# Turning the second group of v by DMA instead of on TensorE, with a split weight load, a wider first fold and later finish steps

## The chip, the cores and the metric

The kernel runs on one core of one Trainium2 chip. The metric is the device time of one execution in microseconds (us). A ratio is the mean time of one kernel's fast runs over that of the kernel before's fast runs of the same rounds, so it is not quite the ratio of the medians that are quoted. The kernel before was timed again with each batch: its medians were 722.87, 723.02 and 723.03 us, so the batches can be laid side by side. A transfer is said to land when the trace records its last completion. Half clock means stretches in which the trace's clock record of TensorE stands at 0.5. Counts of DMA packets by size are taken from the packet records of the traces; no view lists them by size.

## The reference, cut to what matters

```python
# B, N, C = 4, 6080, 256; D_ff = 2048; tau = 1; all float32
qn, kn = q / (norm(q, axis=1) + 1e-6), k / (norm(k, axis=1) + 1e-6)
a = softmax(kn.transpose(0, 2, 1) @ qn / tau)      # 256 x 256 for each b
x = (v @ a).reshape(B * N, C)
r = maximum(x @ w_in, 0)
out = (s * r * r + b) @ w_out
```

## The kernel before

The attention matrix is folded into the first weight, `wa = a @ w_in`, once for each of the four blocks b. After that the work runs over 48 groups of 512 rows of v. A step is one 128-wide part of D_ff: TensorE multiplies `wa` by the turned group `vT` (`mm1`), ScalarE takes the relu, VectorE or ScalarE squares, TensorE multiplies by `w_out`. So each group of v has to be turned first: 128x128 parts with rows and columns exchanged. In the lines below `h_ps` is the result of mm1, `r` its relu, `g` the square, `o_ps` the product with `w_out`, `u` a sum that VectorE makes from `o_ps`, `wa_ps` a piece of the folded weight and `s_ps` the product of k and q for the attention matrix.

```python
def transpose_v(g):                       # on TensorE: 8 transpositions and a copy
    ...
    for j in range(nj):
        for ch in range(CH):
            po(nc.tensor.transpose(vT_ps[:, ch, ts(j, P)], v16[:, j, ts(ch, P)], ident16))
    vT = vtpool.tile([P, CH, TG], FP16, tag="vT", name="vT")
    po(nc.vector.tensor_copy(out=vT[:, :, : nj * P], in_=vT_ps[:, :, : nj * P]))

def crossbar_v(g):                        # by DMA, from SyncE: 4 transfers
    ...
    for j in range(nj):
        po(nc.sync.dma_start_transpose(out=vT[:, :, ts(j, P)], in_=v16[:, j, :]))
```

Groups 0 and 1 are turned on TensorE, all later ones by DMA. The loads of v, w_in, w_out and nearly all of q and k are issued from GpSimd and share its queue; most of them cast from float32 to float16. Their order at the start:

```python
    # ... q and k of block 0 ...
    load_w_in(0, NW)                      # NW = 512
    load_v(0)
    load_w_in(NW, Dff)
    load_v(1)
    # ... w_out in four pieces, load_v(2), scalars; then v3, v4 and q, k of block 1
```

The first `wa` columns are made in pieces, and for later blocks the attention matrix is finished in ten operations placed by the list FIN; one of them, `join` (L266), adds two halves that were turned by DMA (`t_hi`, `t_lo`):

```python
    folds = [fold_both(0, P), fold_both(P, P)]
    folds += [fold_one(2 * P, NW - 2 * P, m) for m in range(CH)]
    ...
    FIN = (-12, 0, 3, 3, 5, 7, 13, 15, 17, 20)   # sqrt, norms, recip, exp, hi, lo, join, exps, exps, sums
```

Of the kernel before, what the change touches and what calls it, by code (L numbers as in the profile page):

```python
# [16 lines left out]
def kernel(  # L17
# [13 lines left out]
    P = 128  # L31

    B, N, C = q.shape
    Dff = moe_w_in.shape[1]
# [19 lines left out]
    def po(ins):  # L54

        tc.keep_in_program_order(ins)
        return ins
# [30 lines left out]
    def h_tile(name):  # L88
        return ps_h.tile([P, 2, TG], FP32, tag="h_ps", name=name)
# [19 lines left out]
    class Gram:  # L109
# [111 lines left out]
        def finish_ops(self):  # L221
# [77 lines left out]
            def scaled(f0, n, m, wa_ps):  # L299
                dst = self.wa[:, m, ds(f0, n)]  # L300
                if m == 0:
                    po(nc.scalar.mul(out=dst, in_=wa_ps, mul=st["rs"][:, m : m + 1]))
                else:
                    po(nc.vector.tensor_scalar_mul(
                        out=dst, in0=wa_ps, scalar1=st["rs"][:, m : m + 1]))

            def fold_mm(f0, n, m, wa_ps):
                for j in range(CH):
                    po(nc.tensor.matmul(wa_ps, st["e"][:, j, ts(m, P)],  # L309
                                        w_in16[:, j, ds(f0, n)],  # L310
                                        start=(j == 0), stop=(j == CH - 1)))

            def fold_both(f0, n):
                def f():

                    two = [self.bank("wa_ps", CH, C)[:, 0, :n], h_tile("wa_ps")[:, 0, :n]]
                    for m in range(CH):
                        fold_mm(f0, n, m, two[m])
                    for m in range(CH):
                        scaled(f0, n, m, two[m])  # L320
                return f

            def fold_one(f0, n, m):
                def f():
                    wa_ps = self.bank("wa_ps", CH, C).rearrange("p a c -> p (a c)")[:, :n]
                    fold_mm(f0, n, m, wa_ps)
                    scaled(f0, n, m, wa_ps)
                return f

            if self.b == 0:  # L330

                folds = [fold_both(0, P), fold_both(P, P)]
                folds += [fold_one(2 * P, NW - 2 * P, m) for m in range(CH)]
            else:
                folds = []
# [16 lines left out]
    def group(g):  # L352
        t0 = g * TG
        return t0, min(TG, NT - t0) // P
# [3 lines left out]
    def load_v(g):  # L358
        t0, nj = group(g)
        v16 = vpool.tile([P, TG // P, C], FP16, tag="v16", name="v16")  # L360
        po(nc.gpsimd.dma_start(  # L361
            out=v16[:, :nj, :],
            in_=v_flat[t0 : t0 + nj * P, :].rearrange("(p j) c -> p j c", j=nj)))
        v_tiles[g] = v16

    def transpose_v(g):
        _, nj = group(g)
        v16 = v_tiles.pop(g)
        vT_ps = ps_o.tile([P, CH, TG], FP16, tag="o_ps", name="vT_ps")
# [5 lines that stand above are left out]
        vT_tiles[g] = vT  # L375

    def crossbar_v(g):

        _, nj = group(g)
        v16 = v_tiles.pop(g)  # L380
# [3 lines that stand above are left out]
        vT_tiles[g] = vT  # L384
# [22 lines left out]
    NW = 512  # L407
    w_in_rows = moe_w_in.rearrange("(co p) f -> p co f", p=P)

    def load_w_in(f0, f1):  # L410
        po(nc.gpsimd.dma_start(out=w_in16[:, :, f0:f1], in_=w_in_rows[:, :, f0:f1]))

    load_w_in(0, NW)
    load_v(0)
    load_w_in(NW, Dff)
    w_out_rows = moe_w_out.rearrange("(fo p) d -> p fo d", p=P)
    load_v(1)

# [37 lines left out]
    fin = g0.finish_ops()  # L456
# [4 lines left out]
    keep_busy(4, w_in16[:, 0, :P], w_in16[:, 0, :NW])  # L461
    fin[5]()
    transpose_v(0)
    for f in fin[6:13]:
        f()


# [44 lines left out]
    def at_step(s, f):  # L512
        side.setdefault(int(s), []).append(f)


    FIN = (-12, 0, 3, 3, 5, 7, 13, 15, 17, 20)
    first_group = [b * N // TG for b in range(B)]
    FOLDS = (0, 0, 3, 4, 7, 8)
    for i, f in enumerate(fin[13:]):
        at_step(FOLDS[i], f)  # L520
    at_step(14, lambda: po(nc.vector.tensor_scalar_mul(
        out=s_out, in0=s_bc, scalar1=1.0 / (LAM * LAM))))
# [14 lines left out]
    for g in range(NG):  # L537
        if g >= 3:
            at_step(max(g - 4, 0) * FT + 2, lambda g=g: load_v(g))
        if g >= 1:  # L540
            if g == 1:
                at_step(12, lambda g=g: transpose_v(g))
            else:
                at_step((g - 2) * FT + 6, lambda g=g: crossbar_v(g))
    for b in range(1, B):
# [21 lines left out]
        def fin_step(gr=gr, s=w1 - fin_len):  # L567
            ops = gr.finish_ops()
            for i, f in enumerate(ops):
                at_step(int(s) + 1 + (FIN[i] if i < 10 else FIN[9] + 3 + (i - 10) * 3), f)  # L570
        at_step(w1 - fin_len - 12, fin_step)
# [224 lines left out]
    for s in range(NS + FT):  # L796
        g, m = divmod(s, FT)
# [66 lines left out]
```

## Time and profile before

| | before |
|---|---|
| time, median of 3 (range) | 722.93 us (722.61 to 723.24) |
| TensorE busy | 700.3 us of the 721.1 us span |
| VectorE, ScalarE busy | 626.3, 544.6 us |
| TensorE idle from 80 us to the end of the steady part | 1.7 us, once, near 164 us |

TensorE is the bound, so the useful question is where it stands still. Besides the lines that the prediction shows, one view is needed: the busy time of each engine in chosen stretches. Its columns are the stretch, its length, then busy us (number of instructions) of PE, PEld, DVE, ACT and POOL, the granted clock of TensorE as a share of full speed, the busy share of the DMA engines and GB/s. Of the kernel before:

```profile
50.00:60.00 10.00, 9.47 (x59) 5.66 (x58) 9.17 (x18) 9.76 (x11) 0.84 (x2) 1.00 1.02 155
60.00:80.00 20.00, 19.37 (x173) 13.47 (x171) 18.91 (x29) 18.08 (x25) 4.44 (x9) 1.00 1.01 167
```

In the stretch where the second group begins (51.8 us), TensorE, ScalarE and VectorE are all nearly full and the clock is full; the DMA engines are full as well (1.02).

### The profile page before, as it was taken

To read this page: it belongs to the slowest core of one execution; us is meant where nothing else is said; L and a number is where in the kernel's file an instruction comes from. 1 tells how busy PE (TensorE), PEld (TensorE's weight loads), DVE (VectorE), ACT (ScalarE), POOL (GpSimd) and SP (SyncE) were. 2 spreads that over 40 slices of the span, in tenths; PEclk is the share of its full clock that TensorE was granted. 3 is DMA by queue.
4 is the path that set the end of the run, shared out by engine and by line. 5 is a ranking of instruction groups with operands and counts; after the bars stand their busy time and mean duration, and the time that the engine had idled before them with its cause. 6 is when DMAs were issued, how large, how long until landed. Compare 5 with 4: busy or idle time off the path is not lost.

```text
span 721.1 us, 17651 instructions
## 1 busy us (share of the span) xinstructions
PE 700.3 (97%) x7485; PEld 505.4 (70%) x7485; DVE 626.3 (87%) x880; ACT 544.6 (76%) x589; POOL 109.1 (15%) x188
## 2 busy tenths in 40 slices
PE   4799999999999999999999999999999999999998
PEld 3556777776677777777677777777668777777777
DVE  4779999988889999999788898999888888888886
ACT  4479877887777777788777777878877777777875
POOL 4522331201101222110210222110000000000000
PEclk9999999999999999999999999999999999999999
DMA  9999998637474989353864777953423333321202
GB/s 236 208 259 140 176 174 141 110 103 126 97 118 105 154 146 141 80 118 78 144 134 89 129 135 131 159 93 83 103 64 78 89 75 74 97 59 45 83 30 75
DMA packets 89519, 84.27 MB, mean 117 GB/s; under 512 B 59648, under 2 KB 64576, under 8 KB 89440
## 3 DMA queue, kind: packets, MB, share of 16 engines
q0 software_dynamic: 25792, 43.40, 37.2%
q1 hardware_dynamic: 63072, 38.43, 21.3%
q8 instruction: 59, 0.97, 0.6%
q10 hardware_dynamic: 576, 1.31, 0.5%
q14 instruction: 20, 0.16, 0.1%
HBM read 78.91 MB, written 24.90 MB: 144 GB/s over the span
## 4 chain that ended last, share of the span: by engine, by line
PE 90%; DMA 5%; DVE 1%; ACT 1%; POOL 1%; issue 1%; DVEq 0%; ACTq 0%; POOLq 0%
PE h_ps L604 44%; PE o_ps L772 39%; PE s_ps L142 4%; PE wa_ps L309 2%; DMA qk<-in_q_dram 2%; DMA w_in<-in_moe_w_in_dram 1%; DMA qk<-in_k_dram 1%; ACT r L614 1%; DMA t_lo<-s_lo 1%; POOL qk L126 1%; PE o_ps L650 0%; PE o_ps L676 0%; ACT g L625 0%; DVE o_sb L632 0%; DVE S L698 0%
## 5 line engine op out<-in xcount | busy, mean ns | idle before, releaser
L614 ACT ACTIVATE r<-h_ps 128x1024 f16<-128x1024 f32 (+1 forms) x384 | 387.8, 1014 | 148.2 <-PE h_ps L604 146.3
L604 PE MATMUL h_ps<-vT,wa 128*128 128x512 f16 (+7 forms) x1632 | 451.9, 364 | 0.6 <-ACT r L614 0.4
L772 PEld LDWEIGHTS <-S 128*128 128x128 f16 x2944 | 197.9, 98 | 85.1 <-issue 0.4
L772 PEld LDWEIGHTS <-g 128*128 128x128 f16 x2208 | 155.0, 98 | 74.1
L627 DVE TENSOR_TENSOR g<-r 128x2048 f16<-128x2048 f16 (+2 forms) x150 | 174.5, 1164 | 16.9 <-ACT r L614 16.9
L772 PE MATMUL o_ps<-T,S 128*128 128x128 f16 x2208 | 183.2, 219 | 0.3 <-DVE S L698 0.2
L604 PEld LDWEIGHTS <-wa 128*128 128x128 f16 x1632 | 136.1, 98 | 23.0 <-issue 2.8
L772 PE MATMUL o_ps<-w_out,g 128*128 128x128 f16 x1472 | 134.2, 219 | 2.0 <-DVE u L632 2.0
L632 DVE SCALAR_TENSOR_TENSOR o_sb<-o_ps,s_out,u 128x256 f32<-128x256 f32 x138 | 66.3, 480 | 45.3 <-PE o_ps L772 42.2
L625 ACT ACTIVATE g<-r 128x1024 f16<-128x1024 f16 (+1 forms) x97 | 100.4, 1035 | 0.2
L142 PE MATMUL s_ps<-qk 128*128 128x256 f16 (+1 forms) x384 | 70.4, 284 | 13.7 <-ACT qk L133 8.9
L361 POOL DMA_DIRECT2D v<-in_v_dram x48 | 31.3, 656 | 266.1 <-DMA vT<-v 222.1
L632 DVE SCALAR_TENSOR_TENSOR u<-o_ps,s_out,rowconst 128x256 f32<-128x256 f32 x138 | 65.8, 476 | 0.0
L772 PE MATMUL o_ps<-w_out,S 128*128 128x128 f16 x736 | 63.5, 219 | 0.0
L772 PE MATMUL o_ps<-N,g 128*128 128x128 f16 x736 | 63.4, 219 | 0.0
L188 POOL DMA_DIRECT2D f<-f x30 | 26.3, 876 | 225.0 <-DVE f L178 199.3
L165 ACT ACTIVATE sq<-qk 128x1024 f16<-128x1024 f16 (+3 forms) x49 | 50.4, 1033 | 11.6 <-DMA qk<-in_k_dram 7.6
L700 DVE TENSOR_TENSOR S<-S,g 128x2048 f16<-128x2048 f16 (+1 forms) x47 | 56.4, 1200 | 1.2
L698 DVE TENSOR_TENSOR S<-g 128x2048 f16<-128x2048 f16 (+1 forms) x47 | 56.0, 1191 | 0.0
L704 DVE TENSOR_TENSOR S<-g,S 128x2048 f16<-128x2048 f16 x46 | 55.9, 1214 | 0.0
L702 DVE TENSOR_TENSOR S<-g 128x2048 f16<-128x2048 f16 x46 | 55.8, 1214 | 0.0
L142 PEld LDWEIGHTS <-qk 128*128 128x128 f16 (+1 forms) x384 | 33.1, 102 | 19.6 <-DVE qk L132 8.3
(75 smaller groups left out, 323.6 us busy)
## 6 DMA issues: line engine op xcount, KB each, us to landing
out_dram<-o_sb SPq DMA_DIRECT2D x46, 512.0 KB, 3.1
v<-in_v_dram POOLq DMA_DIRECT2D x47, 256.0 KB, 4.6
qk<-in_k_dram POOLq DMA_DIRECT2D x42, 256.0 KB, 5.9
qk<-in_q_dram POOLq DMA_DIRECT2D x42, 256.0 KB, 7.2
f<-f POOLq DMA_DIRECT2D x30, 128.0 KB, 3.1
vT<-v SPq DMA_TRANSPOSE x182, 3.2
w<-in_moe_w_out_dram POOLq DMA_DIRECT2D x4, 512.0 KB, 11.6
raw<-in_q_dram ACTq DMA_DIRECT2D x2, 512.0 KB, 6.7
```

The lines of the kernel that those rows point to most:

```text
L142: po(nc.tensor.matmul(self.s_ps[:, ch, :], kc[:np_, j, ts(ch, P)], qc[:np_, j, :], start=(c == 0 and j == 0 and ch == 0), stop=(c == len(s ...
L165: po(nc.scalar.activation(out=st["sq"][:np_, 1, js, :], in_=kc[:np_, js, :], func=AF.Square))
L604: po(nc.tensor.matmul(dst, wa[:, ci, ts(m, P)], src, start=(ci == 0), stop=(ci == CH - 1), skip_group_check=True))
L614: po(nc.scalar.activation(out=r16[:, :, i % 2, :n], in_=h_tiles.pop((g, i))[:, :, :n], func=AF.Relu))
L625: po(nc.scalar.activation(out=dst, in_=src, func=AF.Square))
L627: po(nc.vector.tensor_mul(dst, src, src))
L632: po(nc.vector.scalar_tensor_tensor(out=dst, in0=src, scalar=s_out, op0=ALU.mult, in1=add, op1=ALU.add))
L698: po(nc.vector.tensor_add(T[1], A21, A22))
L700: po(nc.vector.tensor_sub(T[2], T[1], A11))
L702: po(nc.vector.tensor_sub(T[3], A11, A21))
L704: po(nc.vector.tensor_sub(T[4], A12, T[2]))
L772: po(nc.tensor.matmul(st[name][:, j, :], a()[:, i, ts(j, P)], w[:, i, :], start=first, stop=last, skip_group_check=True))
```

## The change

The intent: load the piece of w_in that is needed first by itself, make the first fold in one 256-wide piece, give `t_lo` two steps more before it is joined, and take the eight transpositions of the second group from TensorE and give them to the DMA.

```diff
-                folds = [fold_both(0, P), fold_both(P, P)]
+                folds = [fold_both(0, 2 * P)]
...
-    load_w_in(NW, Dff)
+    load_w_in(NW, 2 * NW)
+    load_w_in(2 * NW, Dff)
...
-    for f in fin[6:13]:
+    for f in fin[6:12]:
...
-    FIN = (-12, 0, 3, 3, 5, 7, 13, 15, 17, 20)
+    FIN = (-12, 0, 3, 3, 5, 7, 15, 17, 19, 22)
-    for i, f in enumerate(fin[13:]):
+    for i, f in enumerate(fin[12:]):
...
-                at_step(12, lambda g=g: transpose_v(g))
+                at_step(0, lambda g=g: crossbar_v(g))
```

## The prediction

Half clock after the wait at +0.5 us was my guess and not worked out from the trace. The sum came to +3.2 us with that term in it: +4.4 for the wait, +0.5 for half clock, -1.7 for the stall.

> **What bounds the kernel now.** I first read the page's busy shares and the chain of work that ended last, to learn which engine sets the end. One line of busy shares and two of the chain:
>
> ```profile
> PE 700.3 (97%) x7485; PEld 505.4 (70%) x7485; DVE 626.3 (87%) x880; ACT 544.6 (76%) x589; POOL 109.1 (15%) x188
> ...
> PE 90%; DMA 5%; DVE 1%; ACT 1%; POOL 1%; issue 1%; DVEq 0%; ACTq 0%; POOLq 0%
> ```
>
> TensorE is the bound: 90% of the chain lies on it. Busy time by stretches of 40 us gives 40.00 of 40 for nearly all of 80 to 700 us. So a change helps only where TensorE is still idle or where it does avoidable work; I searched for those places with the list of waits and the chain in order of time (columns: start, length, what).
>
> The waits of TensorE after the start are few (total us, times, longest):
>
> ```profile
> PE o_ps L772 <- DVE u L632: 2.0, 2, 1.7
> PE wa_ps L309 <- DMA w_in<-in_moe_w_in_dram: 0.4, 1, 0.4
> PE h_ps L604 <- ACT r L614: 0.4, 1, 0.4
> ```
>
> The first is really a DMA: in VectorE's own rows the sum of the turned halves (L266) waits 1.8 us for the last `t_lo` transposition in block 1, and everything behind it in VectorE's order, including the `u` for which TensorE waits, is late. The chain shows the same:
>
> ```profile
> 158.62 4.04 DMA t_lo<-s_lo
> 162.66 0.03 issue
> 162.69 0.05 DVEq L266
> 162.74 0.04 issue
> 162.78 0.65 DVE t_sb L266
> ```
>
> In blocks 2 and 3 the join does not wait (in block 2 its input lands at 335.3 us and it runs at 335.4).
>
> The chain near the first two groups of v is where the rest of the change acts:
>
> ```profile
> 29.96 10.42 DMA w_in<-in_moe_w_in_dram
> 40.38 0.05 issue
> 40.42 1.04 PE wa_ps L309 x4
> ...
> 49.33 0.45 PE vT_ps L372 x8
> 49.77 0.45 PE h_ps L604 x2
> 50.22 0.02 issue
> 50.24 1.02 ACT r L614
> ```
>
> TensorE stands until the 768 KB second piece of w_in lands at 40.38; it then runs without a gap to 50.2, with the eight PE transpositions of the second group of v (L372) inside; from 50.24 to 59.6 the chain lies on ScalarE.
>
> [...] The trace agrees with sharing: the transpositions of v's third group, issued at 48.8 among the loads, need 8.3 and 7.3 us to land, against 2.3 to 2.4 us for one issued at 157 us, when nothing else moves:
>
> ```profile
> vT<-v SPq DMA_TRANSPOSE x1, 8.3
> ```
>
> The trace's packet records give more: after the issue at 48.83 the first 256-byte packet of a transposition moves only at about 52.6; from 52.75 to 54.5 there are 165 of them beside 149 of 2048 bytes from GpSimd's queue, so about one for one, some 90 per us each. One 128x256 transposition is 256 such packets; four are 1024.
> [...] the first s_ps matmuls, after 6.9 us of idle, take 409 ns each against 284 on the average of that row. In the stretches after that I see no cold matmuls. This matters for a stall of several us.
>
> **The change part by part.** The built program's order of instructions confirms each.
>
> 1. *First folds: 256 columns at once instead of two times 128.* TensorE issues 8 `wa` matmuls of 256 columns in place of 8 of 128 and 4 of 256. In columns that is the same work, 2048. ScalarE and VectorE each scale two 256-wide pieces rather than two of 128 and one of 256, so each drops one instruction (VectorE 0.61 us for its two of 128, 0.48 for one of 256: 0.1 us less). The first mm1 waits for a 256-wide piece, about 0.1 us longer to scale than one of 128, and has 0.2 us less to wait for buffers. Net about 0 to 0.1 us; and whatever it saves is then waited for w_in in any case unless part 2 holds.
>
> 2. *w_in's second load cut into 256 KB and 512 KB.* 256 KB loads land 1.25 us apart (v's second group at 41.64, 1.26 after w_in). So the first third should land at about 40.38 - 2 x 1.25 = 37.9 us, before TensorE asks for it (39.4 plus two matmuls of 0.215: 39.85). The fold moves from 40.42 to 39.85: 0.57 us gained. The rest still lands at about 40.4, needed at 42.0.
>
> 3. *Second group of v turned by DMA.* Eight PE transpositions disappear, 0.44 us of TensorE (49.16 to 49.61, back to back), with one VectorE copy of 0.69 us. Before, ScalarE waited 1.20 us for TensorE just there, so the 0.44 us is on the path. With part 2, TensorE would come to the second group's first mm1 at 51.78 - 0.57 - 0.44 = 50.77. But now vT comes over the queue: v's second group lands at 41.64, the four transpositions are issued at about 41.7 to 46.8 (1.27 us each), and until about 56 us GpSimd's queue always has some 8 loads outstanding. With the 3.7 us delay seen at 48.83, the first packet moves at about 45 us; 1024 packets at 90 per us are 11.4 us: 56.4 us for the last one. GpSimd's own packets left at that time, 1019 from 44.5 on, run out no sooner, so the transposition gets no free run. **Estimate: vT ready at 56.5 us, TensorE stands still for 5.7 us.** ScalarE began the first relu of this group at 53.0; now it begins at 56.5 + 0.9 (four matmuls) = 57.4. Cost against before: 4.4 us; the 0.57 and 0.44 us gained are swallowed by this wait. ScalarE, which carries the chain there, executes in order and cannot use the gap. [...]
>
> 4. *The later finish_ops two steps later (15, 17, 19, 22).* A step is about 0.82 us at 157 us of the trace; in the new order VectorE does S L703 (1.2 us) and a `u` before the join, which so comes at about 162.5 rather than 161.0, while its input lands at 162.7. The `u` no longer sits behind it. Gain: the 1.7 us stall. Blocks 2 and 3 had none and gain nothing; their last fold comes at step 47 of 54, so being later costs nothing.
>
> Sum: +4.4 + 0.5 - 1.7 = +3.2 us at the estimate of 56.5. Weighed with the milder cases below, about +2: 722.9 + 2.1 = **725.0 us**.
>
> **The rivals.**
> - *The transposition is hidden (10%).* It lands before 50.8. For it: it is issued some 9 us ahead, and undisturbed ones land in 2.4. Against: every one among deep loads in this trace took 4 to 9 us, and the fourth is issued only at 45.5. Then all the gains count: -0.57 - 0.44 - 1.7 = -2.7, 720.2 us.
> - *It lands in the order of issue (25%).* Many transpositions land just after the load issued shortly before them: those issued from 48.83 land at 57.1 to 58.6, the q load of 49.10 at 56.84. Loads issued up to 45.7 land by about 52.6 in the trace, so vT would be ready at about 53; relu at 53.9, +0.9 - 1.7 = -0.8: 722.1 us.
> - *Shared one for one (55%)*, the account above: 725 to 727.
> - *Shared, and a cold array or delayed loads on top (10%).* vT at 58 or later, half clock, casts of w_out late: 728 or more. Against it: the w_out pieces land by 47.8, needed from 47.1 on, one at a time; the next loads wait for transpositions in both kernels, until 59.2 before, so they are hardly delayed.
>
> **Range and chances.** The cases above spread from 720 to 729; 80% lies in 720.2 to 728.0. 2% is 14.5 us, far more than any account gives: within 2% 0.985, faster 0.005, slower 0.01.
>
> **What would show it.** In the profile after: TensorE's waits should have a new entry, h_ps L605 waiting for DMA vT<-v, once, around 50.8 to 56.5; the chain should pass through that DMA. wa_ps should no longer wait for w_in, and the fold of columns 512 to 1023 should start at about 39.9. The wait of o_ps for `u` of 1.7 us at 165 should be gone, and L266 should wait less than 0.4 us. Matmul durations just after 56.5 tell whether the clock fell. I am wrong if vT lands before 51 (then the kernel is about 2.7 us faster), or if TensorE's other waits grow by some us elsewhere in the steady part.

## The result, and the profile after

The changed kernel took 729.35 us (median of 4; 729.31 to 730.51) against 722.87 us: ratio 1.0093, 95% interval 1.0076 to 1.0111. It is slower by 6.5 us, within 2%, and outside the predicted range of 720.2 to 728.0.

The page of the kernel after, busy shares and the chain by engine:

```profile
PE 700.6 (96%) x7473; PEld 504.9 (69%) x7473; DVE 625.3 (86%) x878; ACT 544.7 (75%) x588; POOL 109.8 (15%) x189
...
PE 90%; DMA 6%; DVE 1%; POOL 1%; ACT 1%; SPq 1%; issue 1%; POOLq 0%; ACTq 0%
```

Shares over the whole span say next to nothing here: DMA went from 5% to 6% of the chain. TensorE has 12 matmuls fewer and yet 0.3 us more busy time, a hint that some of them ran slowly. The list of TensorE's waits of the kernel after (total us, times, longest) shows the change at once:

```profile
...
PE h_ps L605 <- DMA vT<-v: 7.6, 1, 7.6
PE s_ps L142 <- DMA qk<-in_q_dram: 5.4, 7, 1.1
PE h_ps L605 <- ACT r L615: 0.4, 1, 0.4
PE o_ps L773 <- DVE u L633: 0.3, 1, 0.3
...
```

The first line shown is new: one wait of 7.6 us for the turned second group. Waits of `wa_ps` for w_in are gone from the list, and that of `o_ps` for `u` fell from 2.0 to 0.3 us. The chain of the kernel after in order of time (start, length, what) goes through the new wait:

```profile
41.74 1.28 SPq L383
...
46.44 11.87 DMA vT<-v
58.31 0.14 issue
58.45 1.86 PE h_ps L605 x4
```

The four transpositions are issued from 41.74 us on, as soon as v has landed; the fourth, issued at 46.44, takes 11.87 us to land. The landing records give 49.91, 52.57, 55.44 and 58.31 us for the four. Then four matmuls take 1.86 us, where four such take 1.03 us elsewhere. The stretches of the kernel after show the same loss and its second part:

```profile
50.00:60.00 10.00, 2.37 (x10) 0.97 (x9) 8.54 (x16) 2.00 (x3) 1.25 (x4) 0.76 1.18 195
60.00:80.00 20.00, 19.40 (x134) 12.45 (x133) 10.99 (x18) 17.39 (x21) 3.11 (x6) 0.95 0.55 89
```

TensorE worked 2.37 us of ten instead of 9.47, and the granted clock is below 1: the clock record has half speed from 55.3 to 62.1 us. After 80 us the kernels run alike, except that the stall near 164 us (172 in the new count) is gone.

The account closes. The first relu of the second group began at 60.35 us instead of 53.0; in the wait ScalarE did nothing for 8.35 us, though all pieces of w_out, one of which it cast next (61.27 us), had landed by 48.03: it kept to the program's order. Where TensorE next waits 0.4 us for ScalarE, at 59.67 us before and 67.83 us after, the kernel is 8.16 us late. The line of ScalarE after, and those two of TensorE, first before and then after (start, length, what, count, [idle before, releaser]):

```profile
60.35 1.02 ACT L615 ACTIVATE r<-h_ps 128x1024 f16<-128x1024 f32 x1 [8.35 <-PE h_ps L605]
...
59.67 0.59 PE L604 MATMUL h_ps<-vT,wa 128*128 128x512 f16 x2 [0.40 <-ACT r L614]
...
67.83 0.59 PE L605 MATMUL h_ps<-vT,wa 128*128 128x512 f16 x2 [0.40 <-ACT r L615]
```

The later stall gives 1.7 us back, and the spans differ by 727.6 - 721.1 = 6.5 us.

### The profile page after: what moved, and what is told of

The parts are those of the page before. It is cut to its first block, busy times and chain, and to the rows that moved or that the text cites. A ratio compares the mean times of both kernels' runs of the same rounds, so it can differ in the third digit from the quotient of the medians.

```text
span 727.6 us, 17633 instructions
## 1 busy us (share of the span) xinstructions
PE 700.6 (96%) x7473; PEld 504.9 (69%) x7473; DVE 625.3 (86%) x878; ACT 544.7 (75%) x588; POOL 109.8 (15%) x189
## 4 chain that ended last, share of the span: by engine, by line
PE 90%; DMA 6%; DVE 1%; POOL 1%; ACT 1%; SPq 1%; issue 1%; POOLq 0%; ACTq 0%
PE h_ps L605 44%; PE o_ps L773 39%; PE s_ps L142 4%; DMA qk<-in_q_dram 3%; DMA vT<-v 2%; PE wa_ps L309 1%; DMA v<-in_v_dram 1%; SPq L383 1%; POOL qk L126 1%; PE o_ps L651 0%; PE o_ps L677 0%; ACT r L615 0%; ACT g L626 0%; DVE o_sb L633 0%; DVE sq L162 0%
```

## The experiments

My theory: the whole loss is the wait for the DMA transposition, made long by sharing the DMA engines packet for packet with GpSimd's loads, plus the half clock that the wait brings; the other parts gain about 2.3 us. Rivals: other parts of the change cost time; the transposition is slow by itself, or only issued late; the clock costs nothing because ScalarE carries the chain there.

### e1_pe_turn: only the DMA transposition undone

```diff
-                at_step(0, lambda g=g: crossbar_v(g))
+                at_step(12, lambda g=g: transpose_v(g))
```

> The changed kernel with the second group of v turned on TensorE again (step 12), all else kept. My theory (the whole loss is the wait for the DMA transposition plus the half clock behind it): no wait of h_ps for vT, a gain of 0.6 us from the earlier w_in piece and of 1.7 us from the later join, so about 720.5 us, faster than both kernels. Rival (the later finish steps, the wide fold or the split load lose some of the time themselves): above 722.9 us.

Measured 720.38 us (5 runs), ratio 0.9965 (0.9952 to 0.9979). This is the lowest median, below both kernels. So the DMA transposition costs 729.35 - 720.38 = 9.0 us, and the rival that other parts lose time falls.

### e2_crossbar_only: only the DMA transposition done

```diff
-                at_step(12, lambda g=g: transpose_v(g))
+                at_step(0, lambda g=g: crossbar_v(g))
```

> The kernel before with only the second group of v turned by DMA. My theory: vT lands at 58 to 59 us, as in the changed kernel, TensorE waits about 7 us for it and runs 3 to 4 us at half clock; the 1.7 us stall of block 1 stays. About 722.9 + 8.2 = 731 us. Rival (the three other parts are what costs): within 1 us of 722.9.

Measured 732.06 us (4 runs), ratio 1.0125. TensorE waited 7.2 us for vT, which landed at 58.65 us; half clock from 55.7 to 62.5. From its list of waits:

```profile
PE h_ps L604 <- DMA vT<-v: 7.2, 1, 7.2
```

Added alone, the part costs 9.0 us, as much as taking it out gains.

### e3_fin_only: only the later finish steps

```diff
-    FIN = (-12, 0, 3, 3, 5, 7, 13, 15, 17, 20)
+    FIN = (-12, 0, 3, 3, 5, 7, 15, 17, 19, 22)
```

> The kernel before with only the four later finish steps. My theory: the one stall of 1.7 us at 163 to 165 us is gone, nothing else moves: 721.2 us. Rival (the stall only moves to another place, or the later folds hold the next block up): 722.4 us or more.

Measured 720.83 us (5 runs) against 723.02, ratio 0.9970 (0.9958 to 0.9983): a gain of 2.2 us (by the interval 1.2 to 3.0), which is not told apart from the stall of 1.7. TensorE's wait for `u` fell to 0.3 us, and TensorE is busy for 40.00 of the 40 us from 160 on.

### e4_split_and_fold_only: only the split load and the wider fold

```diff
-                folds = [fold_both(0, P), fold_both(P, P)]
+                folds = [fold_both(0, 2 * P)]
...
+    load_w_in(NW, 2 * NW)
+    load_w_in(2 * NW, Dff)
```

> The kernel before with only the split load of w_in and the 256-wide first fold. My theory: TensorE starts the fold of columns 512 to 1023 at 39.75 instead of 40.42 us and passes the 0.6 to 0.7 us on to the end: 722.2 us. Rival (ScalarE carries the chain from 50 to 60 us and swallows it): 722.8 us.

Measured 723.20 us (5 runs: 722.54 to 724.30), ratio 1.0003 (0.9990 to 1.0015): no gain, so my 722.2 was wrong. The profiled run, which is the 724.30 one, shows where it went. TensorE's timeline in block 1 (start, length, what, count, [idle before, releaser]):

```profile
164.62 0.22 PE L773 MATMUL o_ps<-w_out,g 128*128 128x128 f16 x1 [2.05 <-DVE u L633]
164.68 0.59 PE L605 MATMUL h_ps<-vT,wa 128*128 128x512 f16 x2
165.10 0.55 PE L773 MATMUL o_ps<-w_out,g 128*128 128x128 f16 x7
165.50 0.99 PE L605 MATMUL h_ps<-vT,wa 128*128 128x512 f16 x2
166.28 0.95 PE L773 MATMUL o_ps<-w_out,g 128*128 128x128 f16 x7
```

The stall for `t_lo` is still there in this kernel, 2.05 us instead of 1.70. That is not where the gain was lost: the last transposition of `t_lo` was issued at 157.85 us, 0.77 us earlier than in the kernel before (158.62), so the gain had come as far as that. (In this trace 0.33 us of it stood already at the first piece of w_in, which landed at 35.16 instead of 35.49; in e1's trace, without such luck, the issue is 0.66 us earlier.) But the transfer took 4.37 us to land instead of 4.04, and the stall follows that: in e2, where it took 3.95 us, the stall was 1.50. From 165.6 to 169.0 us the array then ran at half clock, so that a pair of `h_ps` matmuls took 0.99 instead of 0.59 us; half of 3.41 us, 1.7, is my estimate of the cost. -0.77 + 0.35 + 1.7 = +1.3 us, and the span is 722.4 - 721.1 = 1.3 us longer. That one run is thus explained. A run of the kernel before, 724.68 us with the same clock of 0.997, looks like it, but left no trace. Of the other four runs, with a clock of 0.999 to 1.0, two took 722.5 us and two 723.2. The nine runs of the kernel before lie in the same two places (three at 722.5 to 722.6, six at 722.8 to 723.2), so this scatter is not e4's own; its cause is open, and beside it a gain of 0.6 us cannot be told from none by these runs. e1 has these two parts and e3 has not, and e1 is 0.45 us faster, but their intervals overlap.

### e5_v1_early: the second group loaded one place earlier

```diff
     load_v(0)
+    load_v(1)
     load_w_in(NW, 2 * NW)
     load_w_in(2 * NW, Dff)
...
-    load_v(1)
```

> The changed kernel with the second group of v loaded one place earlier than the second w_in piece, so that it lands near 37.9 instead of 41.7 us; the same bytes follow behind it. My theory (each transposition needs about 2.8 us while packets of GpSimd's queue alternate with its own, and the four run one behind the other): vT moves earlier by the same 3.8 us, to 54 to 55 us, and the time falls by about 3.8 to 4.5 us to 725 us; w_in's piece lands at 39.2, still in time. Rival A (landing waits for the backlog of loads as a whole to run out): vT still lands at 57 to 58.5 us and the time stays above 728. Rival B (undisturbed transpositions, only the issue is late): vT lands before 45 us and the time is 720.2.

Measured 727.01 us (4 runs), ratio 1.0050. v landed at 37.84 us, 3.9 us earlier, and vT at 55.24 instead of 58.31. So the landing moves with the issue, by 3.1 of the 3.9 us: rival A (the whole backlog must run out) and rival B (only the issue was late) both fall. In the packet records transpositions again share: from 49 to 56 us 626 packets of 256 bytes move beside 616 of 2048 bytes. The time fell by 2.3 us, less than the landing, and the timeline of TensorE says why:

```profile
55.38 1.86 PE L604 MATMUL h_ps<-vT,wa 128*128 128x512 f16 x4 [4.54 <-DMA vT<-v]
57.03 1.06 PE L676 MATMUL o_ps<-w_out,g 128*128 128x256 f16 x4
```

The wait is 4.54 us, but half clock lasts until 61.35 us, 6.1 us past the landing, against 3.8 in the changed kernel. That difference is chance. In the clock records of both runs half clock lasts 6.83 us, two stretches of 3.41 us (see the last section). In the changed kernel vT landed at 58.31 us, just before the first of them ended (58.70); in e5 it landed at 55.24, 0.7 us after the first began (54.52). The length of half clock also varies from run to run: e5's fastest run, 725.95 us, has a granted clock of 0.998 instead of 0.995, which fits one stretch of half clock instead of two, and the slowest of the changed kernel, 730.51 us, has 0.993, which fits three (estimates: twice the missing share of the span is 2.9, 7.3 and 10.2 us).

### e6_three_v_buffers: less traffic beside the transposition

```diff
-    vpool = pool("vpool", 4)
+    vpool = pool("vpool", 3)
```

> The changed kernel with three instead of four buffers for v. The load of v's fifth group then waits for the transpositions of the second, and holds the k and q loads behind it back, so that GpSimd's queue runs empty near 51 us instead of 58. Theory (shared packets): the remaining packets of the transpositions then move at several times the rate, vT lands at 52.5 to 54.5 us, the time is 723 to 725 us. Rival (the transposition itself is slow, whatever else moves): vT still at 58 us, 729 us or more. A third possibility: the wait gets shorter but the held-back loads of k and q are then late for block 1 and cost it again.

Measured 722.11 us (4 runs), ratio 0.9984, better than my 723 to 725. Here GpSimd cannot issue the load of v's fifth group, and so none behind it, before the second is turned. The transpositions were issued at the same times as in the changed kernel, and their first packet moved at the same time (46.1 us in both); they landed at 50.73, 51.43, 51.73 and 51.93 us. The last three followed within 1.2 us of the first, GpSimd's queue having run empty at 50.3 us, instead of 2.7 to 2.9 us apart. So the transposition is not slow by itself (51.93 instead of 58.31 us for the last, with the same issue times). TensorE's timeline:

```profile
52.06 1.02 PE L605 MATMUL h_ps<-vT,wa 128*128 128x512 f16 x4 [1.24 <-ACT r L615]
```

The wait is 1.24 us and the four matmuls take 1.02 us: full clock. (The view names ScalarE as the releaser; the fourth transposition landed at 51.93, just before.)

### e7_keep_busy: dummy matmuls in the wait

```diff
+        if s == FT:
+            idle2 = ps_o.tile([P, TG], FP32, tag="o_ps", name="idle2")
+            for _ in range(30):
+                po(nc.tensor.matmul(idle2, w_in16[:, 0, :P], w_in16[:, 0, :NW],
+                                    start=True, stop=True, skip_group_check=True))
```

> The changed kernel with 30 dummy matmuls of 512 columns (6.5 us) put in front of the second group's first matmul, so that the array isn't idle during the wait; they end at about 57.2 us, before vT lands. Theory (part of the loss is the half clock after the wait, some 1.9 us by the trace): the matmuls after 58.3 us take 379 ns and the time falls by 1 to 2 us to about 727.5. Rival (ScalarE carries the chain there, so the clock costs nothing): 729.3.

Measured 727.79 us (4 runs: 727.62 to 727.83), 1.56 us less than the changed kernel, with vT landing no earlier (58.51):

```profile
50.80 6.64 PE L802 MATMUL idle<-w_in 128*128 128x512 f16 x30
58.64 1.02 PE L605 MATMUL h_ps<-vT,wa 128*128 128x512 f16 x4 [1.21 <-DMA vT<-v]
```

So the half clock cost 1.6 us by itself; the rival that it costs nothing falls.

### e8_half_half: two quarters by DMA, two on TensorE

```diff
-                at_step(0, lambda g=g: crossbar_v(g))
+                at_step(0, lambda g=g: half_dma(g))
+                at_step(12, lambda g=g: half_pe(g))
```

Their definitions are left out: `half_dma` is `crossbar_v` for j = 0 and 1, `half_pe` is `transpose_v` for j = 2 and 3.

> The changed kernel with two of the four quarters of v's second group turned by DMA and two on TensorE (step 12). In the changed kernel the second quarter landed at 52.57 us. Theory: vT is whole at about 52.5 us, TensorE waits 1.5 to 2 us instead of 7.6 and keeps its clock; time 721.5 to 722.5. Rival (one slow landing of any DMA transposition, not the number of packets): vT at 57 or later, 728 or more.

Measured 722.21 us (4 runs), ratio 0.9986, as expected. The second transposition landed at 52.66 us, TensorE waited 1.71 us and kept its clock:

```profile
52.80 1.02 PE L622 MATMUL h_ps<-vT,wa 128*128 128x512 f16 x4 [1.71 <-DMA vT<-v]
```

So the landing follows the number of packets, and is not one late moment for every transposition.

### e9_v1_first: a transposition that is hidden

```diff
+    load_v(1)
     for c in range(NDIRECT, len(g0.chunks)):
         g0.load(c)
...
-    load_v(1)
```

> The changed kernel with the second group of v loaded ahead of all of GpSimd's loads of q and k, so that its DMA transposition is done long before it is needed. Theory (the transposition isn't free even when hidden, since the start waits for loads all the time): no wait of h_ps for vT, but everything up to 36 us comes later by the 1.25 us of the load and by some of the packets' own time (1024 of about 26 ns over 16 engines, 1.7 us), so 720.4 - 0.4 + 1.3 to 3.0 = 721.3 to 723.0 us. Rival (a hidden transposition costs nothing and saves TensorE 0.44 us): 720.0 or less, which would be the fastest kernel here.

Measured 722.74 us (6 runs), ratio 0.9994. vT landed at 25.90 us and nobody waited for it, yet this kernel is 2.4 us slower than e1. The first piece of w_in, the end of the loads that the start waits for, landed at 38.29 instead of 35.43 us, 2.86 us later: v's 1.25 us, and 1.6 us, close to the 1.7 us that the expectation estimated for the packets of the transposition. (It took 26 ns for each; in the changed kernel's trace the packets of 256 bytes take 24.7 ns on average, which makes 1.6 us for 1024 over 16 engines, an estimate.) As this start waits for loads, the hidden transposition was paid there.

### e10_pe_turn_three_buffers: a control that failed

```diff
-    vpool = pool("vpool", 4)
+    vpool = pool("vpool", 3)
...
-                at_step(0, lambda g=g: crossbar_v(g))
+                at_step(12, lambda g=g: transpose_v(g))
```

> Control for the run with three buffers for v: the second group turned on TensorE, three buffers. If the buffers alone cost nothing, it equals the run with four, 720.4 us, and the 722.1 us with the DMA transposition are its remaining wait of 1.2 us and what follows. If three buffers cost time of their own: 721.5 us or more.

Measured 726.97 us (4 runs), ratio 1.0052. It is no control: in this order of the program the fifth group's load is issued only at 56.13 us, just after the third group's last transposition landed at 55.57, and not at 52.49 as in e6. The loads of q and k for block 1 sit behind it, TensorE waited 3.3 us for them, and half clock followed from 62.6 to 69.4. So whether three buffers alone cost e6 anything rests on e6's own trace, in which TensorE waits nowhere else anew. By accident the run shows transpositions of v with nearly nothing beside them. The issues between 49 and 54 us, with size or count and us to landing:

```profile
vT<-v SPq DMA_TRANSPOSE x4, 2.4
```

Against this the same view of the changed kernel, issues from 41 to 47 us:

```profile
vT<-v SPq DMA_TRANSPOSE x4, 9.9
```

Alone, the four landed 6.3 us after the first was issued (49.30 to 55.57); among the loads it took 16.6 us.

### The runs side by side

| run | vT landed, us | TensorE waited, us | half clock past the landing, us | time, us | over e1, us |
|---|---|---|---|---|---|
| e1, on TensorE | - | none | none | 720.38 | 0 |
| e6, three buffers | 51.93 | 1.2 | none | 722.11 | 1.7 |
| e8, half by DMA | 52.66 | 1.7 | none | 722.21 | 1.8 |
| e5, loaded earlier | 55.24 | 4.5 | 6.1 | 727.01 | 6.6 |
| e7, dummy matmuls | 58.51 | 1.2 + 6.6 busy with dummies | none | 727.79 | 7.4 |
| the changed kernel | 58.31 | 7.6 | 3.8 | 729.35 | 9.0 |

Without half clock the time over e1 is the wait, to within 0.5 us; with it, 1.4 to 2.1 us more.

## Why the prediction was right or wrong

The prediction was wrong in its number: 729.35 us lay 1.35 us above the range. Its mechanism was right, a transposition that shares the DMA engines one for one with GpSimd's loads and lets TensorE wait. The step that failed is the size of that wait in part 3, 7.6 us where it had 5.7, and next to it the cost of half clock, 1.6 us where it had 0.5. Its own account before weighing (+3.2 us, so 726.1) was nearer than the 725.0 that it gave.

- **Part 3, vT ready at 56.5 us: mis-sized, 58.31.** The sharing was right: from 49 to 56 us, 624 packets of 256 bytes moved beside 624 of 2048 bytes, 89 per us each. Two ends were too short. I let the first packet move at "about 45 us"; it moved at 46.05, 4.3 us after the issue. And I took the 1024th packet for the landing: in order of time it began to move at 56.85 (the 1024 took 10.8 us, not 11.4), but the fourth transposition landed only at 58.31, 1.46 us later. For the three before it the landing came 0.7 to 0.9 us after the 256th, 512th and 768th packet. Behind the fourth, packets of the third group's transpositions (issued from 49.32 us) followed, and the records do not say whose a packet is, so the 1024th in time need not be the fourth's last. The step "the transposition gets no free run" held: GpSimd's packets moved until 57.4 us. So the wait was 7.6 us and not 5.7.
- **Half clock, +0.5 in the sum: mis-sized, 1.6 us** by e7. The 0.5 was a guess: the trace had no example of a wait of this length in the steady part, and I discounted it because ScalarE carried the chain there. But ScalarE waits for TensorE's matmuls, and they took nearly twice as long (1.86 us for four instead of 1.03): behind its first relu it cast, and then waited 0.73 us for TensorE again (at 63.03 us). How much of half clock is left when vT lands is also a matter of chance (3.8 us here, 6.1 in e5).
- **The weighing.** The two rivals with vT at or before 53 us had 35% of the weight and pulled the estimate down by 1.1 us. Landing "in the order of issue" did not hold: the q load issued at 46.84 landed at 55.16, the transposition issued at 46.44 only at 58.31.
- **Part 1 and part 2, right in place.** TensorE came to the first mm1 at 39.31 instead of 39.41, and to the fold of columns 512 to 1023 at 39.75 (I said 39.85) instead of 40.42; the piece landed at 37.91 (37.9). TensorE would have come to the second group's first mm1 at about 50.65 us (50.77). As I said, in the changed kernel this was swallowed by the wait. Alone (e4) it showed no gain in the times, where I had expected 722.2 us, though the traces of e4 and e1 have it still at 158 us.
- **Part 4, right.** 1.7 us in the account of the changed kernel, and 2.2 us (1.2 to 3.0) alone (e3). The join of block 1 waited 0.23 us, under the 0.4 that I allowed.
- **Two readings of the lines were wrong, without effect on the sum.** GpSimd did not have "some 8 loads outstanding" until 56 us: in the trace before it had 8 until 46, then 6 at 50, 3 at 53 and 1 at 56; so few were enough to keep the sharing going. And slow matmuls did not end with the first ones: those from 8 to 12 us still took 415 ns on average, and the clock record is at full speed only from 15.5 us on.
- **The chances.** Within 2% had 0.985, and that held.

The excess over my own account of 3.2 us adds up: at the common point (67.83 us) the kernel was 8.16 us late where I had 4.9. Of the 3.3 us, 1.8 are the later landing; 1.1 lie between landing and first relu (2.04 us where I had 0.9) and 0.8 up to the common point, less the 0.5 that I had counted for the clock.

## What to carry to other kernels

A transfer that takes 2.4 us in quiet (e10) took 9.9 here, where its small packets alternated with a full queue's large ones. Estimate it as its packets at the pace of the alternation (here about 90 per us), and add the delay before its first packet (4.3 us here) and the one between its last packet and the landing (0.7 to 0.9 us where it could be read). Taking 0.44 us from the bounding engine is worth nothing if its input then comes over a path that is already full (the DMA engines' share was 1.18 from 50 to 60 us); moving the second group back to TensorE and keeping the rest gave the lowest median, 720.4 us. A short wait for a DMA is worth removing: the one for `t_lo` lasted 1.50 to 2.05 us in three traces, and where it lasted 2.05 us half clock followed and cost nearly as much again (e4; 1.7 us by my estimate there).

## What the traces show of the clock and the queues

- In e4 half clock (165.6 to 169.0 us, with matmuls of twice the usual spacing) followed a wait of only 2.05 us. The wait of 1.70 us in the kernel before brought none, nor did 1.71 us in e8. In the clock records the changes lie at whole multiples of 3.41 us from where full speed is first reached (44 of them in e4, 12 and 14 in the changed kernel). Cut into such stretches, by the profile's modelled ends, TensorE was idle for all of the one before half clock in the changed kernel (51.88 to 55.29 us) and in e5 (51.11 to 54.52), and for 60% of it in e4; it was idle for 50% of the one around the 1.70 us. Where between these the line lies, or whether it is the idle share that counts, these runs do not settle. In the changed kernel TensorE was idle for 93% of the first stretch of half clock and never in the second, behind which full clock came back; in e5 it was idle for 0.85 us of the first (54.52 to 57.94 us), and half clock lasted for one stretch more. So the lengths of half clock, 3.41 us in e4 and 6.83 us in the changed kernel and in e5, are one and two stretches.
- A transposition's 256-byte packets and the 2048-byte packets of GpSimd's queue moved one for one in the changed kernel (624 to 624 in 7 us), so the queue of small packets moved an eighth of the other's bytes. Whether the queues took turns after each packet or after several, these counts do not tell.
- The delay before the first packet was 4.3 us beside a full queue (issue 41.74, first packet 46.05) against 1.3 us in quiet (e10: 49.30, 50.56). What causes it, no run here settles.
- Four 128x256 float16 transpositions of 64 KB, alone, took 6.3 us from issue to landing (e10), 42 GB/s. They were issued 1.3 us apart, which by itself allows only about 50 GB/s (estimate: 64 KB in 1.3 us).
